# Seven tiles of a q-k product as three single-pass products from high and low parts, with the low parts made on GpSimd

## The chip, the cores and the metric

One core of one Trainium2 chip runs the whole program. The metric is the device time of one execution in microseconds (us). PE is TensorE, DVE is VectorE, ACT is ScalarE, POOL is GpSimd, and SP is the queue that issues most of the loads.

## The reference

All inputs are float32. The core of what is computed:

```python
# q, k, v: (1, 6016, 256); tau: a number; w_in (256, 2048), w_out (2048, 256), twice
qn = q / (np.linalg.norm(q, axis=1, keepdims=True) + 1e-06)
kn = k / (np.linalg.norm(k, axis=1, keepdims=True) + 1e-06)
s = kn.transpose(0, 2, 1) @ qn / tau          # 256 x 256, a sum over 6016 tokens
a = softmax of s over its last axis
x = v @ a                                     # 6016 x 256
h = x @ w_in;  g = h * (1.0 / (1.0 + np.exp(-1.702 * h)));  y = g @ w_out
h = y @ w2_in; g = np.where(h > 0.0, h, np.exp(np.minimum(h, 0.0)) - 1.0);  out = g @ w2_out
```

The norms run over the 6016 tokens, so a column of q or k has one norm, and the division by it can be made on the 256 x 256 product.

## The kernel before, in words

The program has two parts. The first, some 50 us long, loads q and k and makes the product, the norms and the softmax. The second, the long one, runs the two MLPs in units of 448 or 512 tokens; the change doesn't touch it. Each engine runs its instructions in the order in which the code writes them.

**The first part.** The 6016 tokens are 47 tiles of 128. `CHUNKS` cuts them into 17 chunks: 1, 2, 1, 2, 2, 2 tiles, then 3 and 4 alternately five times, then 2. Chunk 6 is the first of 3 tiles and chunk 7 the first of 4; chunk 16 is the last one. For a chunk, SP loads its q and k (`load_qk`), ACT squares both at once (L768), DVE adds the squares up (L638, through `sums`), and PE makes the product (L680, `gram`). The product s has two halves of 128 rows, each in a PSUM bank: `gram(i, c)` adds the tiles of chunk i to half c. Its operands are float32, and PE makes each of these products in two passes, each of them a record of its own in the trace.

- **The sums of squares.** From chunk 6 on, DVE folds a chunk's 3 or 4 tiles of squares into 2 (the sum into `sq`) and adds these into `pair` (128 x 1024). The squares lie in three buffers, so the squares of a chunk wait until the sums have read those three chunks back. From chunk 14 on, the additions into `pair` are made in halves of 512 columns, eight in all, and then two additions make `acc` (128 x 256 each for q and k).
- **The order on PE.** Up to chunk 11 both halves of a chunk are made at once. From chunk 12 on (`SPLIT`) half 0 is made for all five chunks, then half 1 of chunk 12 and of two tiles of chunk 13. Then stands `norms()` (L692): four tiny products that sum `acc` over the partitions. The rest of half 1 (11 tiles) and the transposes of v (L452) are written between the steps of the softmax, to fill PE while the other engines work.
- **The steps of the softmax.** `norms()` is read by an ACT copy (L696), a GpSimd power (L697, square roots of 4 columns) and DVE (L700, L701, reciprocals); PE then spreads the reciprocal norms of q over the partitions (L709, `rows_of_q`, it reads `rn`), and ACT copies that from PSUM to `rq` (L713). DVE multiplies half 0 by both norms (L719, `lowest(0)`), takes row minima (L723), ACT takes exponentials (L728), PE transposes them (L739), and the result is multiplied into the first weights (L541, `fold_half`). tau comes through L813 on PE and L702 on DVE. In the same places DVE and ACT unpack the weights of the MLP (L213, L217, L225, L228, L231, L267, L273).

GpSimd has, in the first 100 us, a few fills at the start and the power of 4 columns.

Of the kernel before, what the change touches and what calls it, by code (L numbers as in the profile page):

```python
# [9 lines left out]
F32 = mybir.dt.float32  # L10
# [7 lines left out]
P = 128  # L18
# [4 lines left out]
def kernel(  # L23
# [40 lines left out]
    nc = tc.nc  # L64
    _, NT, C = q.shape
# [3 lines left out]
    NJ = NT // P  # L69
# [11 lines left out]
    SPLIT = 12  # L81
# [48 lines left out]
    def x_tile(kind, b, i):  # L130
        x_t[kind, b, i] = xp.tile([P, 2, BANK], F32R, tag=f"x{i}", name=f"x{kind}")
        return x_t[kind, b, i]
# [237 lines left out]
    def do(f, n):  # L370
        f(n)
        if f in (split, split_lo):
            state["done"] = n
# [237 lines left out]
    with tc.manual_schedule():  # L611
        make_identity(nc, ident)

        with ExitStack() as st:
# [11 lines left out]
            starts = [sum(CHUNKS[:i]) for i in range(NC)]  # L626
            MM = max(CHUNKS)
            s_ps = bank[:KC]

            qk = [wts.tile([P, 14 * C], F32, tag=f"wA{i}", name="qk") for i in range(4)]  # L630

            def warm_up(n):
                for _ in range(n):
                    one = nc.const_aps.tensor(1.0, [P, P], F32)
                    nc.tensor.matmul(bank[3][:, :P], one, one, start=True, stop=True)  # L635

            def add(out, x, y):
                return lambda: nc.vector.tensor_add(out, x, y)  # L638

            def halves(y):  # L640
                return [add(pair[:, x], pair[:, x], y[:, x]) for x in range(2)]

            def sums(i, sq):

                m = CHUNKS[i]
                if i < 3:
                    kept.append(sq)
                    if not i:
                        return []
                    lone, two = kept[i - 1 and 2], kept[1]  # L650
                    return [add(pair[:, :, i - 1, :], two[:, :, i - 1, :], lone[:, :, 0, :])]
                a = sq[:, :, :2, :]
                if i in (3, 4, 5):
                    return [add(pair, pair, a)]
                if i == NC - 2:
                    return halves(a) + halves(sq[:, :, 2:, :])
                if m == 4:
                    return [add(a, a, sq[:, :, 2:, :]), add(pair, pair, a)]
                if m == 3:
                    x = sq[:, :, 0, :]  # L660
                    if i == NC - 3:
                        return [add(x, x, sq[:, :, 2, :])] + halves(a)
                    return [add(x, x, sq[:, :, 2, :]), add(pair, pair, a)]
                return halves(a) + [
                    add(acc[:, x], pair[:, x, 0, :], pair[:, x, 1, :]) for x in range(2)
                ]
# [6 lines left out]
            rk = ph1.tile([P, KC], F32, name="rk")  # L673
            rq_ps = bank[3][:, C:]
            e, rq = pair[:, 0], pair[:, 1, 0, :]

            def gram(i, c, cut=slice(None)):
                t = chunk[i]
                for s in range(CHUNKS[i])[cut]:
                    nc.tensor.matmul(  # L680
                        s_ps[c][:, :C],
                        t[:, 1, s, c * P:(c + 1) * P],
                        t[:, 0, s, :],
                        start=(starts[i] + s == 0),
                        stop=(starts[i] + s == NJ - 1),
                    )

            def norms():
                for i in range(2):
                    for c in range(KC):  # L690
                        x = i * KC + c
                        nc.tensor.matmul(  # L692
                            n_ps[:, x:x + 1], acc[:, i, c * P:(c + 1) * P], ones[:, 0:1],
                            start=True, stop=True,
                        )
                nc.scalar.copy(rn, n_ps[:, :2 * KC])  # L696
                nc.gpsimd.tensor_tensor(rn, rn, half, op=ALU.pow)  # L697
# [9 lines left out]
            def rows_of_q():  # L707
                for c in range(KC):
                    nc.tensor.matmul(  # L709
                        rq_ps[:, c * P:(c + 1) * P], rn[:, c:c + 1].to_broadcast([P, P]), ident,  # L710
                        start=True, stop=True,
                    )
                nc.scalar.copy(rq, rq_ps)  # L713

            mn = ph1.tile([P, KC], F32, name="mn")
            sm = ph1.tile([P, KC], F32, name="sm")

            def lowest(c):
                nc.vector.scalar_tensor_tensor(  # L719
                    out=e[:, c, :], in0=s_ps[c][:, :C], scalar=rk[:, c:c + 1], in1=rq,  # L720
                    op0=ALU.mult, op1=ALU.mult,
                )
                nc.vector.tensor_reduce(  # L723
                    mn[:, c:c + 1], e[:, c, :], axis=AX.X, op=ALU.min
                )

            def exps(c):
                nc.scalar.activation(  # L728
                    e[:, c, :], e[:, c, :], AF.Exp, bias=mn[:, c:c + 1], scale=-1.0,
                    accum_out=sm[:, c:c + 1],  # L730
                )
# [17 lines left out]
            def load_qk(i):  # L749
                m, a = CHUNKS[i], i % 2  # L750
                t = qk[i // 2 % 4][:, :8 * C] if a else qk[i // 2 % 4][:, 8 * C:]
                t = t.rearrange("p (x s c) -> p x s c", x=2, c=C)
                j = starts[i]
                nc.sync.dma_start(out=t[:, 0, :m, :], in_=qv[:, j:j + m, :])
                (nc.scalar if i < 3 else nc.sync).dma_start(out=t[:, 1, :m, :], in_=kv[:, j:j + m, :])
                return t
# [3 lines left out]
            chunk = []  # L760
            warm_up(6)
            for i, m in enumerate(CHUNKS):
                t = first[i] if i < 4 else load_qk(i)
                chunk.append(t)
                sq = gp.tile([P, 2, MM, C], F32, tag="g", name="sq")
                cuts = (slice(0, 2), slice(2, m)) if i == NC - 2 else (slice(0, m),)
                for x in cuts:
                    nc.scalar.activation(sq[:, :, x, :], t[:, :, x, :], AF.Square)  # L768
                todo += sums(i, sq)
                if todo:  # L770
                    todo.pop(0)()
                while len(todo) > 1:
                    todo.pop(0)()
                if i < SPLIT:
                    for c in range(KC):
                        gram(i, c)
                if i == 0:
                    warm_up(1)
# [13 lines left out]
            def turn_v(c, h):  # L792
                transpose_v(0, h, c, bank[4 + 2 * h + c])

            for i in range(SPLIT, NC):
                gram(i, 0)
            gram(SPLIT, 1)
            gram(SPLIT + 1, 1, slice(0, 2))
            do(scale, 0)
# [2 lines left out]
            do(join, 0)  # L802
            do(sign, 0)
            do(shift, 1)
            norms()
            turn_v(0, 0)
            gram(SPLIT + 1, 1, slice(2, None))
# [6 lines left out]
            inverse()  # L814
            do(split_lo, 0)
            rows_of_q()
            gram(SPLIT + 2, 1, slice(2, None))
            gram(SPLIT + 3, 1, slice(0, 3))
            turn_v(0, 1)
            do(scale_low, 2)  # L820
            lowest(0)
            exps(0)
            do(sign, 1)
            sums_inverse(0)
# [6 lines left out]
            gram(SPLIT + 4, 1)  # L831
            fold_half(0, 0, bank[3][:, :C])
            lowest(1)
            half_out(0, 0, bank[3][:, :C], 0)
            exps(1)
# [616 lines left out]
        for t in range(len(units) + 1):  # L1452
            u = units[t] if t < len(units) else None
            if u:
                kind, b, p = u
# [78 lines left out]
```

## Time and profile before

| what | value |
|---|---|
| runs of the kernel before | 1036.75, 1037.41, 1037.40 us; median 1037.4 |
| profiled execution, its own time | 1035.95 us |
| its span in the trace | 1034.2 us |
| PE busy over the span | 1029.1 us |
| DVE, ACT, POOL busy | 830.0, 755.9, 65.6 us |
| granted clock of TensorE | 1.00 in every stretch |

The span is what the trace shows from its first to its last instruction; 1.75 us of the execution lie outside it. Ends of matmuls are modelled by the profiler, so PE's busy time says that it is never long without work, and the chain of waits says where it waited.

### The profile page before, as it was taken

Reading aid. Unit: us, or ns where it says so; the run is one execution under the profiler, and the core shown is the slowest. Engines: PE = TensorE matmul, PEld = TensorE weight load, DVE = VectorE, ACT = ScalarE, POOL = GpSimd, SP = SyncE. Lnnn points to the kernel's source line nnn. Section 1 sums busy time; section 2 is a strip of 40 time slices with the busy share of each in tenths; the row PEclk is TensorE's granted clock in tenths of the full one; section 3 lists DMA queues with packets and bytes.
Section 4 is the critical chain, followed back from the end, with each engine's and each line's share of the span. In section 5 each row is a group of like instructions: output and inputs, shape, how many; then the busy total and the mean of one; then the engine's idle time right before and its main releaser. Section 6 shows DMA issues by size and latency. Waiting matters only on the chain.

```text
span 1034.2 us, 13723 instructions
## 1 busy us (share of the span) xinstructions
PE 1029.1 (100%) x4784; PEld 871.3 (84%) x4784; DVE 830.0 (80%) x1352; ACT 755.9 (73%) x1418; POOL 65.6 (6%) x118
## 2 busy tenths in 40 slices
PE   9999999999999999999999999999999999999998
PEld 8899988888888888888888888888888888888998
DVE  6888877757768777767348999998998998998897
ACT  6687676777677677777567878777777777777875
POOL 0000111102102111111000000000000000000000
PEclk9999999999999999999999999999999999999999
DMA  9852663356485586474573132123114024014021
GB/s 361 305 155 61 209 210 112 146 190 223 146 304 188 177 312 228 126 283 183 223 260 127 41 109 96 21 30 155 34 28 143 4 35 145 1 29 138 1 31 47
DMA packets 127543, 145.22 MB, mean 140 GB/s; under 512 B 91218, under 2 KB 94722, under 8 KB 126962
## 3 DMA queue, kind: packets, MB, share of 16 engines
q1 hardware_dynamic: 111554, 87.39, 27.4%
q0 software_dynamic: 15344, 56.17, 14.5%
q8 instruction: 37, 0.61, 0.2%
q10 hardware_dynamic: 576, 0.79, 0.2%
q14 instruction: 32, 0.26, 0.1%
HBM read 86.70 MB, written 57.61 MB: 140 GB/s over the span
## 4 chain that ended last, share of the span: by engine, by line
PE 99%; DMA 0%; ACT 0%; issue 0%
PE b L993 46%; PE b L892 40%; PE b L680 4%; PE b L1020 4%; PE b L583 4%; PE b L541 1%; DMA qk<-in_k_dram 0%; PE b L452 0%; PE b L692 0%; PE b L709 0%; PE b L739 0%; ACT ob L1058 0%; PE b L813 0%; PE b L635 0%
## 5 line engine op out<-in xcount | busy, mean ns | idle before, releaser
L993 PE MATMUL b<-g,wBA 128*128 128x512 f32 (+1 forms) x1152 | 295.9, 385 | 0.0
L892 PE MATMUL b<-xB,wAB 128*128 128x512 f32 (+1 forms) x1008 | 263.7, 385 | 0.0
L993 PEld LDWEIGHTS b<-g,wBA 128*128 128x128 f32 x1152 | 216.2, 188 | 41.1 <-DVE wBA L273 0.3
L993 PE MATMUL b<-g,wBB 128*128 128x512 f32 x960 | 250.1, 389 | 0.0
L892 PE MATMUL b<-xA,wAA 128*128 128x512 f32 x840 | 223.1, 389 | 0.0
L892 PEld LDWEIGHTS b<-xB,wAB 128*128 128x128 f32 x1008 | 187.0, 188 | 34.9 <-DVE b L1311 0.3
L993 PEld LDWEIGHTS b<-g,wBB 128*128 128x128 f32 x960 | 180.0, 188 | 37.5
L892 PEld LDWEIGHTS b<-xA,wAA 128*128 128x128 f32 x840 | 157.6, 188 | 32.9 <-ACT b L1298 0.4
L951 ACT CAST g<-gg 128x512 fp32r<-128x512 f32 (+1 forms) x192 | 117.0, 617 | 81.9 <-DVE gg L944 79.1
L939 DVE SCALAR_TENSOR_TENSOR ee<-ee,th 128x512 f32<-128x512 f32 (+1 forms) x192 | 129.7, 675 | 22.3 <-ACT th L929 22.2
L922 ACT ACTIVATE g<-b 128x512 fp32r<-128x512 f32 (+1 forms) x152 | 89.8, 591 | 75.2 <-PE b L892 66.9
L955 DVE TENSOR_TENSOR g<-gf,g 128x512 fp32r<-128x512 f32 (+1 forms) x192 | 129.1, 674 | 14.6 <-ACT gf L923 14.6
L1311 DVE TENSOR_TENSOR b<-b,s 128x512 f32<-128x512 f32 (+1 forms) x88 | 60.9, 692 | 93.1 <-PE b L892 88.2
L955 DVE TENSOR_TENSOR g<-gg,g 128x512 fp32r<-128x512 f32 (+1 forms) x192 | 127.6, 670 | 5.7 <-ACT g L951 4.1
L928 ACT ACTIVATE ee<-b 128x512 f32<-128x512 f32 (+1 forms) x144 | 84.8, 589 | 35.2 <-PE b L892 35.0
L944 DVE SCALAR_TENSOR_TENSOR gg<-b,ee 128x512 f32<-128x512 f32 (+1 forms) x144 | 98.0, 680 | 5.0
L923 ACT ACTIVATE gf<-b 128x512 f32<-128x512 f32 (+1 forms) x152 | 89.4, 588 | 3.2 <-DVE g L955 3.2
L929 ACT ACTIVATE th<-b 128x512 f32<-128x512 f32 (+1 forms) x144 | 84.1, 584 | 0.0
L1305 ACT COPY s<-b 128x512 f32<-128x512 f32 (+1 forms) x88 | 51.8, 589 | 27.1 <-PE b L892 27.0
L1330 DVE TENSOR_TENSOR c<-b,s 128x512 f32<-128x512 f32 (+1 forms) x88 | 59.8, 679 | 14.7 <-PE b L892 14.4
L1298 ACT COPY b<-b 128x512 f32<-128x512 f32 (+1 forms) x88 | 51.6, 586 | 13.5 <-PE b L892 13.2
L1020 PE MATMUL b<-wBB,g 128*128 128x256 f32 x336 | 46.2, 283 | 0.0
(111 smaller groups left out, 897.0 us busy)
## 6 DMA issues: line engine op xcount, KB each, us to landing
xdA<-xt POOLq DMA_DIRECT2D x35, 512.0 KB, 3.2
xA<-xdA SPq DMA_DIRECT2D x35, 512.0 KB, 5.7
xdB<-xt POOLq DMA_DIRECT2D x35, 512.0 KB, 3.5
xB<-xdB SPq DMA_DIRECT2D x35, 512.0 KB, 5.5
wAB<-w3d SPq DMA_DIRECT2D x4, 1792.0 KB, 8.4
v_raw<-in_v_dram SPq DMA_DIRECT2D x160, 32.0 KB, 2.4
out_dram<-ob SPq DMA_DIRECT2D x160, 32.0 KB, 1.7
raw<-in_moe_w_in_dram SPq DMA_DIRECT2D x8, 512.0 KB, 7.6
```

What stands on the lines that cost most here:

```text
L892: nc.tensor.matmul(dst[:, :n], w[:, wi, p % 2, WOP[kind][i], :], x[:, xi, :n], start=(start and k == 0), stop=(k == 2), skip_group_check=True,
L922: nc.scalar.activation(self.sl(ik)[0], h, AF.Gelu_apprx_sigmoid)
L923: nc.scalar.activation(t[:, :n], h, AF.Gelu_apprx_sigmoid)
L928: nc.scalar.activation(e[:, :n], h, AF.Exp)
L929: nc.scalar.activation(t[:, :n], h, AF.Tanh, scale=0.5)
L939: nc.vector.scalar_tensor_tensor(out=e[:, :n], in0=e[:, :n], scalar=1.0, in1=t[:, :n], op0=ALU.add, op1=ALU.mult,)
L944: nc.vector.scalar_tensor_tensor(out=g[:, :n], in0=h, scalar=0.0, in1=e[:, :n], op0=ALU.max, op1=ALU.min)
L951: nc.scalar.copy(self.sl(ik)[0], self.tmp[ik][:, :self.n])
L955: nc.vector.tensor_sub(lo, self.tmp.pop(ik)[:, :self.n], hi.bitcast(F32))
L993: nc.tensor.matmul(bank[a][:, :n], w[:, f, wi, d * P:(d + 1) * P], g[:, gi, k * n:(k + 1) * n], start=fresh((kind, b, a)), stop=(p == NP - ...
L1020: nc.tensor.matmul(bank[a][:, x * C:(x + 1) * C], g[:, gi, s * P:(s + 1) * P], w[:, f, wi, :], start=fresh((kind, b, a)), stop=(p == NP - ...
L1311: nc.vector.tensor_add(bank[c][:, :n], bank[b][:, :n], s5[:, :n])
```

## The change

Seven tiles (`SPLITS` lists chunk and tile) no longer go through the float32 product. ACT copies q and k of the tile (512 columns) to a single-pass type, the high part; GpSimd subtracts this from the float32 values, which gives the low part; PE makes three single-pass products: high by high, high by low, low by high. The parts lie in seven buffers that the second part of the program uses later (`x_tile`, `SLOTS`). In chunks 8 to 11 ACT's copies stand ahead of the squares of the chunk, in chunk 12 behind them. One of DVE's sums into `sq`, that of chunk 14, goes to GpSimd. ACT copies half 0 of the product to SBUF ahead of the norms, `lowest(0)` reads that copy and the spread norms straight from PSUM, and the copy to `rq` moves behind `lowest(0)`.

```diff
@@ sums
                     if i == NC - 3:
-                        return [add(x, x, sq[:, :, 2, :])] + halves(a)
+                        nc.gpsimd.tensor_add(x, x, sq[:, :, 2, :])
+                        return halves(a)
@@
+            SPLITS = [(8, 2), (9, 2), (9, 3), (10, 2), (11, 2), (11, 3), (12, 2)]
+            SLOTS = [0, 4, 5, 1, 3, 6, 2]
+            split_t = {}
+
+            def split_qk(i):
+
+                for n, (x, s) in enumerate(SPLITS):
+                    if x != i:
+                        continue
+                    y = split_t[i, s] = x_tile("qk", n, SLOTS[n])
+                    hi, lo = (y[:, a, :].rearrange("p (x c) -> p x c", c=C) for a in range(2))
+                    src = chunk[i][:, :, s, :]
+                    nc.scalar.copy(hi, src)
+                    nc.gpsimd.tensor_sub(lo, src, hi.bitcast(F32))
@@ gram
-                    nc.tensor.matmul(
-                        s_ps[c][:, :C],
-                        t[:, 1, s, c * P:(c + 1) * P],
-                        t[:, 0, s, :],
-                        start=(starts[i] + s == 0),
-                        stop=(starts[i] + s == NJ - 1),
-                    )
+                    y = split_t.get((i, s))
+                    terms = [(t[:, 1, s, r], t[:, 0, s, :])]
+                    if y is not None:
+                        k = [y[:, a, C:][:, r] for a in range(2)]
+                        x = [y[:, a, :C] for a in range(2)]
+                        terms = [(k[0], x[0]), (k[0], x[1]), (k[1], x[0])]
+                    for n, (a, b) in enumerate(terms):
+                        nc.tensor.matmul(
+                            s_ps[c][:, :C], a, b,
+                            start=(starts[i] + s == 0 and n == 0),
+                            stop=(starts[i] + s == NJ - 1 and n == len(terms) - 1),
+                        )
@@ rows_of_q
-                nc.scalar.copy(rq, rq_ps)
@@ lowest
+                x, y = (s_ps[1][:, :C], rq) if c else (e[:, 0, :], rq_ps)
                 nc.vector.scalar_tensor_tensor(
-                    out=e[:, c, :], in0=s_ps[c][:, :C], scalar=rk[:, c:c + 1], in1=rq,
+                    out=e[:, c, :], in0=x, scalar=rk[:, c:c + 1], in1=y,
@@ the loop over chunks
+                if i < SPLIT:
+                    split_qk(i)
                 cuts = (slice(0, 2), slice(2, m)) if i == NC - 2 else (slice(0, m),)
                 for x in cuts:
                     nc.scalar.activation(sq[:, :, x, :], t[:, :, x, :], AF.Square)
+                if i >= SPLIT:
+                    split_qk(i)
@@ behind the loop
             do(shift, 1)
+            nc.scalar.copy(e[:, 0, :], s_ps[0][:, :C])
             norms()
@@
             lowest(0)
+            nc.scalar.copy(rq, rq_ps)
             exps(0)
```

On ACT, chunks 8 to 12 of the changed program (`xqk` is the tile of high and low parts, `sq` the squares, `qk` a chunk as loaded; the line numbers of the changed program are higher):

```order
L690 CAST xqk_224<-qk_131 128x512
L792 ACTIVATE sq_223<-qk_131 128x2x768
L690 CAST xqk_243<-qk_131 128x512
L690 CAST xqk_246<-qk_131 128x512
L792 ACTIVATE sq_242<-qk_131 128x2048
L690 CAST xqk_271<-qk_132 128x512
L792 ACTIVATE sq_270<-qk_132 128x2x768
L690 CAST xqk_290<-qk_132 128x512
L690 CAST xqk_293<-qk_132 128x512
L792 ACTIVATE sq_289<-qk_132 128x2048
```

Before, only the `sq` rows stood there, back to back; now six copies stand between them, and a seventh behind the squares of chunk 12.

On GpSimd, from the fills at the start to the first loads that it issues (here `rn` holds the norms):

```order
 L621 MEMSET ones 128x128
 L622 MEMSET half 128x4
-L697 TENSOR_TENSOR rn<-rn,half 128x4
+L691 TENSOR_TENSOR xqk<-qk,xqk 128x512 x7
+L662 TENSOR_TENSOR sq<-sq 128x2x256
+L719 TENSOR_TENSOR rn<-rn,half 128x4
 L188 DMA raw<-in_moe_w_in_dram 128x1024 x2
```

Eight instructions of 512 columns, each with two inputs in SBUF, now stand ahead of the power.

On DVE, the end of the sums of squares, from chunk 13 on:

```order
 L638 TENSOR_TENSOR sq<-sq 128x2x512
 L638 TENSOR_TENSOR pair<-pair,sq 128x1024
-L638 TENSOR_TENSOR sq<-sq 128x2x256
 L638 TENSOR_TENSOR pair<-pair,sq 128x512 x8
 L638 TENSOR_TENSOR acc<-pair 128x256 x2
```

The sum of chunk 14 is gone from DVE, and the first of the eight halves waits for GpSimd instead.

## Rows read from the trace of the kernel before

**Rows 1.** The page: PE's busy time, and the chain that ended last, by engine.

```profile
PE 1029.1 (100%) x4784; PEld 871.3 (84%) x4784; DVE 830.0 (80%) x1352; ACT 755.9 (73%) x1418; POOL 65.6 (6%) x118
PE 99%; DMA 0%; ACT 0%; issue 0%
```

**Rows 2.** The chain of waits, 0 to 50 us: start us, length us, what.

```profile
5.45 34.97 PE b L680 x162
40.42 0.79 PE b L692 x8
...
43.73 0.64 PE b L709 x4
...
46.54 0.35 PE b L739 x2
46.89 1.30 PE b L680 x6
48.18 0.71 PE b L541 x6
```

**Rows 3.** The same view near the end: products of 256 columns, single-pass.

```profile
963.05 1.43 PE b L1020 x12
```

**Rows 4.** The timeline of DVE: start us, length us, instruction, count, idle time before it.

```profile
31.44 1.23 DVE L638 TENSOR_TENSOR sq<-sq 128x1024 f32<-128x1024 f32 x1 [1.04 <-ACT sq L768]
32.70 1.22 DVE L638 TENSOR_TENSOR pair<-pair,sq 128x1024 f32<-128x1024 f32 x1
33.84 0.68 DVE L638 TENSOR_TENSOR sq<-sq 128x512 f32<-128x512 f32 x1
34.56 4.91 DVE L638 TENSOR_TENSOR pair<-pair,sq 128x512 f32<-128x512 f32 x8
39.38 0.76 DVE L638 TENSOR_TENSOR acc<-pair 128x256 f32<-128x256 f32 x2
40.04 0.43 DVE L225 TENSOR_SCALAR bits<-raw 128x512 int32<-128x512 int32 x1
...
41.34 0.69 DVE L231 SCALAR_TENSOR_TENSOR bits<-raw,bits 128x512 int32<-128x512 int32 x1
...
42.51 0.69 DVE L228 CUSTOM_DVE_ANT_0 bits<-raw,bits 128x1024 uint16<-128x1024 uint16 x1
...
43.32 0.18 DVE L701 RECIPROCAL rn<-rn 128x4 f32<-128x4 f32 x1
43.77 0.17 DVE L702 RECIPROCAL rtau<-b 128x1 f32<-128x1 f32 x1 [0.28 <-PE b L813]
...
44.82 0.48 DVE L719 SCALAR_TENSOR_TENSOR pair<-b,rk,pair 128x256 f32<-128x256 f32 x1
```

**Rows 5.** The timeline of ACT.

```profile
19.43 3.45 ACT L768 ACTIVATE sq<-qk 128x2048 f32<-128x2048 f32 x2 [1.08 <-DVE pair L638]
23.95 1.91 ACT L768 ACTIVATE sq<-qk 128x2048 f32<-128x2048 f32 x1 [1.08 <-DVE pair L638]
26.92 1.49 ACT L768 ACTIVATE sq<-qk 128x1536 f32<-128x1536 f32 x1 [1.06 <-DMA qk<-in_k_dram]
29.49 3.44 ACT L768 ACTIVATE sq<-qk 128x2048 f32<-128x2048 f32 x2 [1.08 <-DMA qk<-in_k_dram]
...
42.07 0.62 ACT L267 CAST w1s<-bits 128x512 fp32r<-128x512 f32 x1 [0.67 <-DVE bits L231]
42.60 0.53 ACT L462 CAST xA<-b 128x448 fp32r<-128x448 f32 x1
...
44.41 0.37 ACT L713 COPY pair<-b 128x256 f32<-128x256 f32 x1 [0.72 <-PE b L709]
```

**Rows 6.** The timeline of GpSimd, 0 to 50 us.

```profile
1.02 0.29 POOL masks.py:199 TENSOR_SCALAR_AFFINE_SELECT ident<-ident 128x128 f32<-128x128 f32 x1
...
1.41 0.10 POOL L622 MEMSET half<- 128x4 f32 x1
41.55 1.39 POOL L697 TENSOR_TENSOR rn<-rn,half 128x4 f32<-128x4 f32 x1 [40.05 <-ACT rn L696]
```

More of the change, by code (lines that the diff above doesn't have):

```diff
@@ L675 @@
             e, rq = pair[:, 0], pair[:, 1, 0, :]
+            SPLITS = [(8, 2), (9, 2), (9, 3), (10, 2), (11, 2), (11, 3), (12, 2)]
[10 more added lines that the diff above has]
+                    nc.gpsimd.tensor_sub(lo, src, hi.bitcast(F32))
             def gram(i, c, cut=slice(None)):
                 t = chunk[i]
+                r = slice(c * P, (c + 1) * P)
                 for s in range(CHUNKS[i])[cut]:
-                    nc.tensor.matmul(
-                        s_ps[c][:, :C],
-                        t[:, 1, s, c * P:(c + 1) * P],
-                        t[:, 0, s, :],
-                        start=(starts[i] + s == 0),
-                        stop=(starts[i] + s == NJ - 1),
-                    )
+                    y = split_t.get((i, s))
[10 more added lines that the diff above has]
+                        )
             def norms():
```

## The prediction

> **What bounds the kernel now.** I read the page first. PE is busy for 1029.1 of 1034.2 us, and the chain that ended last lies on PE for 99% of the span [rows 1]. So a product that PE need not make is worth its time, unless another engine then comes late. Second, the chain in order of time [rows 2]: from 5.45 to 40.42 us PE makes q-k products without a break, 162 records in 34.97 us, and after that it goes from step to step of the softmax with hardly a gap. Third, who stands close behind PE there: the timeline of DVE [rows 4]. The second addition into `acc` ends at 39.38 + 0.76 = 40.14 us, and PE begins the norms that read `acc` at 40.42 [rows 2, 4]. From L225 at 40.04 to L701 at 43.32 DVE works almost without a pause, `rn` is there at 43.50, and PE begins to spread it (L709) at 43.73 [rows 2, 4]. DVE is thus within 0.3 us of being the bound at both places. That is the point of the whole case: PE can gain in this stage only what DVE gains too.
>
> **What PE saves.** A record of the float32 product takes 34.97 / 162 = 0.216 us, a product is two records, 0.432 us [rows 2]. A single-pass product of 256 columns takes 1.43 / 12 = 0.119 us near the end of the program [rows 3], and 0.71 / 6 = 0.118 in L541 [rows 2]. Three of them cost 0.358 us, which is 0.074 less than one float32 product. Seven tiles in two halves are 14 products: 14 x 0.074 = 1.0 us. All 14 stand ahead of the norms, so PE would reach the norms at 39.4 instead of 40.42.
>
> **Are the parts there in time?** A copy of 512 columns on ACT costs 0.53 us from start to start (42.07 to 42.60) [rows 5]. GpSimd's price for 512 columns with two inputs is not in the trace. Its rows give 0.29 us for 128 columns with one input and 0.10 for 4 columns [rows 6], hence 0.19 for each further 128 columns read. With one stream that makes 0.10 + 4 x 0.19 = 0.86, with two streams read in turn 0.10 + 8 x 0.19 = 1.62 us. I take the middle, 1.2, and keep both ends. PE makes a tile (both halves) in 0.864 us, so it comes to chunk 8's split tile at about 5.45 + 16 x 0.864 + 0.86 = 20.1 us, to chunk 11's second at about 28.5 and to chunk 12's at about 31.3. ACT's copies of these end at about 17.4, 25.5 and 29.4 (next part), GpSimd's last difference 1.2 us later, chunk 11's at 27.4 because two queue there. Even at 1.62 us each (19.1, 28.2, 31.0) PE does not wait. No cost here.
>
> **What the copies do to ACT and DVE.** ACT has a pause of about 1.08 us ahead of nearly every pair of squares [rows 5], and the copies fill it. Chunk 9 has landed by 19.43 at the latest. Two copies push its squares (1.91 us) to 20.5 to 22.4; a copy and 1.49 us of squares bring chunk 10 to 24.4; two copies and 1.91 bring chunk 11 to 27.4 (before: 25.86); chunk 12's squares end at 28.9 and its copy at 29.4. Chunk 13 starts at 29.49 as before, and ACT is level again [rows 5]. DVE's sums cost, from start to start, 1.26 (sum of 4 tiles), 1.14 (addition into `pair`) and 0.72 (sum of 3 tiles) [rows 4]. Chunk 11's sum can start at 27.4, so chunk 12's starts at 29.8, chunk 13's at 31.7 (before: 31.44), and chunk 13's addition ends its turn at 34.1. There the sum of chunk 14 stood (33.84); it is gone, so the eight halves can begin at 34.1 instead of 34.56, some 0.45 us earlier. They wait for GpSimd's sum: chunk 14's squares end at 29.49 + 3.44 = 32.93 [rows 5], and 1.2 us later is 34.13, just in time. The change thus spends nearly all of what DVE sheds (0.72) and the idle 1.04 us ahead of 31.44 on the late squares, and keeps 0.45.
>
> **The sum.** The additions into `acc` end at 39.7, so PE finds them ready at 39.4 to 39.8, and the norms end 1.0 us earlier than before. But `rn` hangs on DVE, which moves by 0.45 only: L709 starts at 43.73 - 0.45 = 43.28, though PE would be there at 42.73. PE waits 0.55 us and 0.45 of the 1.0 is kept. Behind that DVE gains a little more: its 0.28 us of waiting for tau (L702) vanishes, since PE makes that product early [rows 4]. `lowest(0)` could then start at 44.82 - 0.73 = 44.1. The copy to `rq`, 0.37 us on ACT [rows 5], would have allowed 44.33; the spread norms in PSUM are there at 43.28 + 0.64 = 43.92 [rows 2], so here the rewritten `lowest` helps. The exponentials come 0.73 us earlier, the transposes L739 no longer wait for them (at most 0.1 us of their 0.35 [rows 2]), and PE reaches L541 about 0.5 us before 48.18. The extra copy of half 0 on ACT costs nothing: ACT idles ahead of the norms, and PE needs neither. Were that cover gone it would cost its 0.37 us. Behind 48 us the chain is PE's own work again, and a shift of 0.5 us stays. The profiled execution took 1035.95 us, so 1035.45; the median of the runs lies 1.45 above it, so the forecast is **1036.9 us**. Its own range is a gain of 0.3 to 1.0, 1036.4 to 1037.1. A difference of 0.2% (2.07 us) is about what a measurement of this kernel tells from none, so this counts as no change.
>
> **Rival 1, the end on the other side: GpSimd and DVE shut each other out.** All eight new GpSimd instructions read two tiles in SBUF, while DVE runs one addition with two SBUF inputs after the other. If only one of the two engines can run such an instruction at a time, DVE loses 8 x 1.2 = 9.6 us. Its pauses under the forecast between chunk 8 and the halves take up about 2.2 of that, and the 0.45 and 0.28 above are lost; `acc` and everything behind it come 6.7 us later than before, and PE stands: 1044 us, with the ends 0.86 and 1.62 from 1041.4 to 1047.5. It turns into "slower" once each instruction takes more than about 0.3 us from DVE. For it: nothing in the trace shows DVE and GpSimd both streaming. Against it: the power on GpSimd spans 41.55 to 42.94, L231 (two SBUF inputs) runs from 41.34 into it and L228 starts within it at 42.51, and each takes 0.69 us [rows 4, 6]. That is weak, since the power reads only 4 columns. The Trainium skill, SBUF — State Buffer, section Who interferes with whom, says that a Vector instruction with two SBUF inputs contends with a GpSimd instruction that reads SBUF, by an exclusive lock held for the whole instruction. By that rule the sum would be the 1044 of this rival; the row just told does not agree with a lock over the whole span. I give it 0.19.
>
> **Rival 2, a shared port.** Both go on, each more slowly. If DVE loses half of GpSimd's time, 4.8 us, less the 2.2 of pauses and half of the gain, the end comes 2 to 3 us later: 1039.8, between 1038 and 1041.3. Same evidence; 0.12.
>
> **Rival 3, the change does nothing.** GpSimd's price is the upper end. Its sum of chunk 14 then ends at 32.93 + 1.62 = 34.55, the halves start at 34.56 as before, and PE's 1.0 us turns into waiting at the norms and at L709: 1037.3. For it: the margin in the forecast is nil at 1.2 us. 0.12.
>
> **How the numbers follow.** Forecast 0.54, rival 1 0.19, rival 2 0.12, rival 3 0.12, and 0.03 for a gain over 0.2%, which no row carries, since PE sheds 1.0 us in all. Faster 0.03; same 0.54 + 0.12 + the 0.03 of rival 2 that stays below 2.07 us, 0.69; slower 0.28. The range runs from 1035.9 (all of the 1.0 kept, and half a us of spread between runs) to 1041.3 (all of rival 2): it leaves out rival 1 and the large gain, about 0.2.
>
> **What would show it.** Right: 42 single-pass records in the place of 28; the additions of `acc` end at 39.7; PE idles about half a us at L709; GpSimd's eight instructions last about 1.2 us each and DVE's additions keep 0.69 and 1.23 us. Wrong, if DVE's additions grow longer or wait for GpSimd, if the first of the eight halves starts later than 34.6, or if PE waits for a low part ahead of chunk 12.

## The result, and the profile after

The changed kernel takes 1045.34 us (median of 5 runs, 1044.29 to 1045.75) against 1037.09 for the kernel before (5 runs, 1036.27 to 1037.41). The ratio is 1.0081, 95% interval 1.0069 to 1.0092: slower by 0.8%. The profiled execution took 1045.34 us too, with a span of 1043.6. It was rival 1 that came (1044, between 1041.4 and 1047.5), and not the forecast of 1036.9.

The page of the changed kernel, busy times and the chain by engine, against [rows 1]:

```profile
PE 1033.0 (99%) x4798; PEld 874.2 (84%) x4798; DVE 837.4 (80%) x1351; ACT 759.5 (73%) x1426; POOL 78.8 (8%) x126
PE 95%; DVE 3%; DMA 1%; ACT 0%; issue 0%; SPq 0%; ACTq 0%; DVEq 0%
```

DVE has one instruction less and is busy 7.4 us longer, and the chain that ended last, which was 99% PE, now lies on DVE for 3% of the span. So one looks at how long DVE's instructions last. The timeline of DVE in the changed kernel, against [rows 4]:

```profile
18.06 2.18 DVE L638 TENSOR_TENSOR pair<-pair,sq 128x1024 f32<-128x1024 f32 x1
20.16 1.77 DVE L638 TENSOR_TENSOR sq<-sq 128x512 f32<-128x512 f32 x1
...
30.32 1.23 DVE L638 TENSOR_TENSOR pair<-pair,sq 128x1024 f32<-128x1024 f32 x1
31.47 2.31 DVE L638 TENSOR_TENSOR sq<-sq 128x1024 f32<-128x1024 f32 x1
...
36.81 2.29 DVE L638 TENSOR_TENSOR sq<-sq 128x1024 f32<-128x1024 f32 x1
39.14 6.24 DVE L638 TENSOR_TENSOR pair<-pair,sq 128x1024 f32<-128x1024 f32 x9
45.29 0.76 DVE L638 TENSOR_TENSOR acc<-pair 128x256 f32<-128x256 f32 x2
...
48.43 0.69 DVE L228 CUSTOM_DVE_ANT_0 bits<-raw,bits 128x1024 uint16<-128x1024 uint16 x1
```

And the timeline of GpSimd in the same stretch, against [rows 6]:

```profile
17.50 1.66 POOL L691 TENSOR_TENSOR xqk<-qk,xqk 128x512 fp32r<-128x512 f32 x1 [15.99 <-ACT xqk L690]
20.05 3.01 POOL L691 TENSOR_TENSOR xqk<-qk,xqk 128x512 fp32r<-128x512 f32 x2 [0.90 <-ACT xqk L690]
23.52 1.76 POOL L691 TENSOR_TENSOR xqk<-qk,xqk 128x512 fp32r<-128x512 f32 x1 [0.46 <-ACT xqk L690]
26.06 3.69 POOL L691 TENSOR_TENSOR xqk<-qk,xqk 128x512 fp32r<-128x512 f32 x2 [0.77 <-ACT xqk L690]
30.76 1.93 POOL L691 TENSOR_TENSOR xqk<-qk,xqk 128x512 fp32r<-128x512 f32 x1 [1.02 <-ACT xqk L690]
36.68 1.35 POOL L662 TENSOR_TENSOR sq<-sq 128x512 f32<-128x512 f32 x1 [3.98 <-ACT sq L792]
47.98 1.22 POOL L719 TENSOR_TENSOR rn<-rn,half 128x4 f32<-128x4 f32 x1 [9.95 <-ACT rn L718]
```

Read the two side by side. An addition of 1024 columns that meets no GpSimd instruction keeps 1.23 us, as at 30.32; one that meets one lasts 2.18 to 2.31, and a sum of 512 columns 1.77 in place of 0.69. There are eight such additions for the eight GpSimd instructions, each longer by 0.95 to 1.08 us, 8.2 us in all. Of that DVE's shorter pauses take up 1.4 (its waits for squares from 13.8 us on fall from 3.6 us to 2.2) and the sum it no longer makes 0.7; 6.1 remain. `acc` is complete at 46.05 in place of 40.14, 5.9 us late.

The ends of the rows show that the two engines take turns. GpSimd's first difference ends at 17.50 + 1.66 = 19.16, and the addition that began at 18.06 ends 1.08 us later, at 20.24. The other way round, the addition of 30.32 ends at 31.55, and the difference that began at 30.76 ends 1.14 us later, at 32.69. So it is in all eight meetings: an addition of 1024 columns ends 1.08 us after GpSimd's instruction, a sum of 512 columns 0.55 us after it, and GpSimd's instruction 1.13 to 1.15 us after DVE's. The rows of both engines grow, because they contain the wait for the other.

The timeline of PE shows the two places where it stood, ahead of a low part and ahead of the norms:

```profile
29.80 0.50 PE L704 MATMUL b<-xqk 128*128 128x256 f32 x2 [0.73 <-POOL xqk L691]
...
45.77 1.87 PE L714 MATMUL b<-ones,acc 128*128 128x1 f32 x8 [4.83 <-DVE acc L638]
```

The chain of waits of the changed kernel from there, against [rows 2]:

```profile
45.77 1.87 PE b L714 x8
...
48.59 3.41 PE b L704 x8
...
52.52 1.05 PE b L731 x4
53.57 1.73 PE b L704 x8
...
57.25 0.71 PE b L541 x6
```

L714 is the norms (before L692), L731 spreads the reciprocal norms (before L709). PE reaches L541 at 57.25 in place of 48.18, 9.07 us later, which is the whole loss of the profiled execution (1045.34 - 1035.95 = 9.4) but for 0.3. Of this, 5.35 us are there when the norms begin (45.77 in place of 40.42). The other 3.72 lies in PE's own rows from there to L541: the norms last 1.87 us in place of 0.79, and the eight records of the q-k product at 48.59 last 3.41 in place of 1.73, which is also what the next eight take at 53.57. The view by stretches (length, busy us and records of PE, PEld, DVE, ACT, POOL, then the granted clock, the DMA share and GB/s) says why:

```profile
40.00:50.00 10.00, 5.17 (x21) 4.45 (x20) 9.04 (x18) 5.77 (x11) 1.22 (x1) 0.65 0.50 197
50.00:60.00 10.00, 10.00 (x52) 8.38 (x52) 6.18 (x16) 4.20 (x12) 0.00 (x0) 0.83 0.04 6
```

PE was without work for 4.83 us ahead of the norms, and the granted clock, 1.00 in every stretch of before, is 0.65 and 0.83 in these two. The eight records took 0.426 us each, twice the 0.216 of before, so PE ran at the lower of its levels (1.2 GHz) and came back to 2.4 GHz by 53.57.

### The profile page after: what moved, and what is told of

It is laid out like the page before. It is cut to its first block, busy times and chain, and to the rows that moved or that the text cites. A ratio compares the mean times of both kernels' runs of the same rounds, so it can differ in the third digit from the quotient of the medians.

```text
span 1043.6 us, 13777 instructions
## 1 busy us (share of the span) xinstructions
PE 1033.0 (99%) x4798; PEld 874.2 (84%) x4798; DVE 837.4 (80%) x1351; ACT 759.5 (73%) x1426; POOL 78.8 (8%) x126
## 4 chain that ended last, share of the span: by engine, by line
PE 95%; DVE 3%; DMA 1%; ACT 0%; issue 0%; SPq 0%; ACTq 0%; DVEq 0%
PE b L1021 45%; PE b L920 40%; PE b L1048 4%; PE b L583 4%; DVE pair L638 1%; DVE sq L638 1%; DMA qk<-in_k_dram 1%; PE b L541 1%; PE b L704 1%; PE b L452 0%; ACT sq L792 0%; PE b L714 0%; PE b L731 0%; ACTq L777 0%; SPq L776 0%
## 5 line engine op out<-in xcount | busy, mean ns | idle before, releaser
L492 POOL DMA_DIRECT2D xdB<-xt x42 | 23.8, 567 | 299.7 <-ACT g L979 165.3
```

## The experiments

**Theory A.** An addition on DVE with two inputs in SBUF and a GpSimd instruction that reads two tiles in SBUF shut each other out for most of GpSimd's time; the wait that this gives PE then lets its clock fall. **Rivals.** The copies: ACT's copies hold up the squares, and DVE is late for that reason. The products: the low parts come too late for PE, or the single-pass products cost more than they save. The busy neighbour: GpSimd slows DVE whatever their operands.

**1. No low parts** (`e1_no_low`: the products take the high part three times; GpSimd's sum of chunk 14 stays)

```diff
-                    nc.gpsimd.tensor_sub(lo, src, hi.bitcast(F32))
...
-                        terms = [(k[0], x[0]), (k[0], x[1]), (k[1], x[0])]
+                        terms = [(k[0], x[0]), (k[0], x[0]), (k[0], x[0])]
```

> The low parts aren't made and the three products read the high parts instead, so the low parts are left out of the result; ACT's seven copies, the 42 single-pass products and GpSimd's sum of chunk 14 stay. Theory A (GpSimd and DVE exclude each other): DVE's additions between 17 and 31 us go back to 1.23 and 0.69 us, only the one beside GpSimd's sum of chunk 14 stays long, PE waits under 1 us at the norms, 1036.5 to 1038. Theory B (ACT's copies delay the squares, and with them DVE): the wait at the norms stays at 4 to 5 us, 1043 or more.

1037.93 us, ratio 1.0019 (1.0010 to 1.0029). All additions up to 33 us have 1.23 and 0.69 us again, with ACT's copies and all 42 single-pass products in place. One of them in the timeline of DVE:

```profile
27.95 1.23 DVE L638 TENSOR_TENSOR sq<-sq 128x1024 f32<-128x1024 f32 x1 [1.21 <-ACT sq L791]
```

7.4 of the 8.3 us are gone with seven GpSimd instructions: the copies and the single-pass products fall as the main cause. 0.8 to 1.1 us remain; experiment 7 turns to them.

**2. GpSimd fills the low parts with zeros** (`e2_fill_low`: seven GpSimd instructions of the same size that read nothing)

```diff
-                    nc.gpsimd.tensor_sub(lo, src, hi.bitcast(F32))
+                    nc.gpsimd.memset(lo.bitcast(F32), 0.0)
```

> GpSimd fills the low parts with zeros instead of subtracting, so the low parts are left out of the result; all else as in the change, the same eight instructions on GpSimd, seven of them reading nothing. If it is the reading on GpSimd that shuts DVE out: DVE's additions keep 1.23 and 0.69 us except beside the sum of chunk 14, 1036.5 to 1038. If any GpSimd instruction does, or the handing over between ACT, GpSimd and PE: 1042 or more.

1037.75 us, ratio 1.0014 (1.0005 to 1.0024). But the fills did not run beside the additions. A fill waits for no copy of ACT, and GpSimd made all seven at the start (the timeline of GpSimd), while DVE's first addition begins at 7.06:

```profile
1.44 3.29 POOL L691 MEMSET xqk<- 128x512 f32 x7
```

So this run repeats experiment 1, the change without GpSimd's reading beside DVE's additions, and does not test the busy neighbour. Experiment 5 has fills beside additions.

**3. DVE makes the low parts itself** (`e3_dve_low`)

```diff
-                    nc.gpsimd.tensor_sub(lo, src, hi.bitcast(F32))
+                    nc.vector.tensor_sub(lo, src, hi.bitcast(F32))
```

> DVE makes the low parts itself, GpSimd only the sum of chunk 14. DVE gets 7 x 0.72 = 5.0 us more work, of which about 2 go into pauses. Theory A: each difference on GpSimd cost DVE about 1.0 us, so its own 0.72 is cheaper: acc about 2 to 3 us later than in the kernel before, and less clock lost, 1039 to 1042. Theory C (the port is only shared, the loss is elsewhere): as slow as the change or slower, 1045 or more.

1040.36 us, ratio 1.0038 (1.0023 to 1.0052). The timeline of DVE shows what a difference costs there, and what is left of the meeting with GpSimd (the sum of chunk 14):

```profile
18.26 0.69 DVE L691 TENSOR_TENSOR xqk<-qk,xqk 128x512 fp32r<-128x512 f32 x1
...
33.49 2.30 DVE L638 TENSOR_TENSOR sq<-sq 128x1024 f32<-128x1024 f32 x1
```

A low part costs DVE 0.69 us if it makes it, and 1.03 if GpSimd makes it beside an addition. Handing this work to the idle engine took more of the busy one than doing it there.

**4. The change with PE kept at work ahead of the norms** (`e4_keep_clock`: twenty spare products whose result nobody reads)

```diff
+            warm_up(20)
             norms()
```

> The change with 20 products of constants (128 columns, float32, about 0.22 us each) ahead of the norms, so that PE works while it waits for acc. If the fall of TensorE's clock behind the wait is a cost of its own: the granted clock stays at 1.00 between 40 and 60 us, the products behind the norms go back to their old lengths, 3 to 3.7 us less than the change, 1041.5 to 1042.5. If the long records there are waiting for operands: no difference, 1045.

1043.92 us, ratio 1.0069 (1.0054 to 1.0084), 1.4 us below the change in the medians and above the range expected. The intervals of the two ratios overlap, so the profile has to decide. The stretch of the wait, and L541 in the chain of waits:

```profile
40.00:50.00 10.00, 9.52 (x71) 8.66 (x70) 9.51 (x21) 5.70 (x11) 1.17 (x1) 1.00 0.49 193
```

```profile
53.99 0.71 PE b L541 x6
```

The clock stays at 1.00 (from 50 to 60 us too) and PE reaches L541 3.26 us earlier than in the change, with `acc` as late as there (46.19). So of the 9.07 us in the profiles 3.26 are the clock's and 5.8 DVE's lateness. The runs give back less (two at 1043.0, two at 1044.9); why the latter two are longer, no profile shows.

**5. The pairs by themselves** (`m1_pairs`: a small program, six instructions of each kind on one or both engines, no part of this kernel)

```diff
+        def two(n=2 * N):
+            nc.vector.tensor_add(vc[:, :n], va[:, :n], vb[:, :n])
...
+        def one_psum():
+            nc.vector.tensor_add(vc[:, :N], bk, vb[:, :N])
...
+        def scaled():
+            nc.vector.tensor_scalar(vc[:, :N], va[:, :N], 3.0, None, op0=ALU.mult)
...
+        def pool_two():
+            nc.gpsimd.tensor_sub(pc, pa, pb)
...
+        def pool_copy():
+            nc.gpsimd.tensor_copy(pc, pa)
```

`two` is L97, `one_psum` L100 (`bk` lies in PSUM, all else in SBUF), `scaled` L103, `pool_two` L106, `pool_copy` L112; L109 fills `pc`.

> A program of its own that leaves the whole computation out and copies q to the output: seven stages of up to six DVE and six GpSimd instructions side by side, in this order: GpSimd differences of 512 columns alone; DVE additions of 1024 columns with two SBUF inputs alone; both together; DVE additions of 512 columns with one input in PSUM beside the differences; DVE two-input additions beside GpSimd fills; the same beside GpSimd one-input copies; DVE one-input multiplications of 512 columns beside the differences. Theory A (one at a time): together the third stage takes about 6 x (1.23 + 1.15) = 14 us, records of either engine near 2.3 us; with one input in PSUM and beside fills both keep their own lengths (0.69, 1.23). Theory C (a shared port, both run on): in the third stage both records grow by a part and overlap, 9 to 11 us in all. For the one-input copies and multiplications no theory here has a number; if the second reading port is the cause, the copies exclude the two-input additions too.

The timeline of both engines, six instructions to a row: GpSimd alone, DVE alone, then the pairs.

```profile
23.25 7.96 POOL L106 TENSOR_TENSOR pc<-pa,pb 128x512 f32<-128x512 f32 x6
...
31.86 7.52 DVE L97 TENSOR_TENSOR vc<-va,vb 128x1024 f32<-128x1024 f32 x6
...
40.08 12.23 DVE L97 TENSOR_TENSOR vc<-va,vb 128x1024 f32<-128x1024 f32 x6
40.19 13.23 POOL L106 TENSOR_TENSOR pc<-pa,pb 128x512 f32<-128x512 f32 x6
...
53.95 4.31 DVE L100 TENSOR_TENSOR vc<-bk,vb 128x512 f32<-128x512 f32 x6
...
54.25 7.97 POOL L106 TENSOR_TENSOR pc<-pa,pb 128x512 f32<-128x512 f32 x6
...
62.86 7.53 DVE L97 TENSOR_TENSOR vc<-va,vb 128x1024 f32<-128x1024 f32 x6
62.90 3.43 POOL L109 MEMSET pc<- 128x512 f32 x6
...
71.10 8.96 DVE L97 TENSOR_TENSOR vc<-va,vb 128x1024 f32<-128x1024 f32 x6
71.21 9.33 POOL L112 COPY pc<-pa 128x512 f32<-128x512 f32 x6
```

GpSimd's difference takes 7.96 / 6 = 1.33 us alone, DVE's addition 1.25. Side by side both stretch, and the two sets end after 13.3 us; one whole instruction after the other they would take 15.5. The single rows alternate as in the kernel: each addition ends 1.08 us after a difference, each difference 1.12 after an addition, and six such pairs are the 13.3 us. With one of DVE's inputs in PSUM neither feels the other (4.31 / 6 = 0.72; 7.97). Beside fills the additions last 7.53, as alone (7.52), so it is not GpSimd's being busy: that rival falls. All this is theory A without the kernel around it, except that the two do not exclude each other for quite the whole length of an instruction.

The last stage had no number from theory A: DVE's multiplication of 512 columns with one input, in SBUF, beside differences. Its group by shape (shortest, median and longest in ns, first and last start in us):

```profile
L103 DVE TENSOR_SCALAR vc<-va x6: 426/1366/1369, 81.2 to 87.3; 128x512 f32<-128x512 f32 x6
```

The first, which began ahead of GpSimd, lasted 0.43 us, the other five 1.37. Having only one input in SBUF is thus not enough: this instruction was shut out too, which the addition with one input in SBUF and one in PSUM was not.

**6. Three tiles in place of seven** (`e8_three_tiles`)

```diff
-            SPLITS = [(8, 2), (9, 2), (9, 3), (10, 2), (11, 2), (11, 3), (12, 2)]
-            SLOTS = [0, 4, 5, 1, 3, 6, 2]
+            SPLITS = [(8, 2), (9, 2), (10, 2)]
+            SLOTS = [0, 4, 1]
```

> Three split tiles (the third of chunks 8, 9 and 10) in the place of seven, the sum of chunk 14 on GpSimd as in the change. Theory A: four additions on DVE are longer by about 1.0 us each in the place of eight, of which 1 to 2 us go into pauses, and PE's wait at the norms and the fall of the clock are smaller or absent: 1037.5 to 1039.5. If the loss came from one place (the last chunk's low part, or the sum of chunk 14) and not by the number of instructions: 1043 or more, or no loss at all.

1040.55 us, ratio 1.0032 (1.0023 to 1.0042), 1 us above the range expected. Four GpSimd instructions, four longer additions in the timeline of DVE:

```profile
19.80 2.18 DVE L638 TENSOR_TENSOR pair<-pair,sq 128x1024 f32<-128x1024 f32 x1
21.90 1.77 DVE L638 TENSOR_TENSOR sq<-sq 128x512 f32<-128x512 f32 x1
...
24.85 2.30 DVE L638 TENSOR_TENSOR sq<-sq 128x1024 f32<-128x1024 f32 x1
...
34.45 2.30 DVE L638 TENSOR_TENSOR sq<-sq 128x1024 f32<-128x1024 f32 x1
...
42.93 0.75 DVE L638 TENSOR_TENSOR acc<-pair 128x256 f32<-128x256 f32 x2
```

Half the instructions, half the loss on DVE (4.2 of 8.2 us); `acc` is 3.5 us late, PE waits 2.40 us at the norms, and the granted clock of 40 to 50 us is 0.83. Of the 10 runs the four at 1038.5 to 1039.0 us, with a granted clock of 0.999, lie in the range; the six above it, 1040.3 to 1042.1, have 0.996 to 0.998.

**7. The copies and the products alone, the rewrite alone, the sum alone.** `e7_copies_alone` has no new GpSimd instruction (high parts only, DVE makes the sum of chunk 14). `e5_edit_only` has `SPLITS = []` and that sum on DVE, so only the copies of half 0 and `rq` differ from before. `e6_sum_only` is `e5_edit_only` with the sum on GpSimd. `e12_copies_fill` is `e7_copies_alone` with six spare products ahead of the norms.

```diff
# e7_copies_alone: as experiment 1, and
-                        nc.gpsimd.tensor_add(x, x, sq[:, :, 2, :])
-                        return halves(a)
+                        return [add(x, x, sq[:, :, 2, :])] + halves(a)
# e12_copies_fill: the same, and
+            warm_up(6)
             norms()
```

> As the run without low parts (they are left out of the result), and the sum of chunk 14 is on DVE again, so GpSimd has no new instruction. Theory A: no addition on DVE is longer than 1.23 us, acc ends within 0.5 us of the kernel before, 1036.3 to 1037.3. Theory B (ACT's copies alone cost): over 1038.

> No tile is split and the sum of chunk 14 is on DVE; only the rewritten first row minimum (half 0 copied to SBUF, the spread norms read from PSUM) is left of the change. Every theory: within 0.5 us of the kernel before, 1036.3 to 1037.3, since DVE's weights stand ahead of it in either. If it costs by itself: over 1038.

> GpSimd makes the sum of squares of chunk 14, and nothing else of the change is there. Theory A: one VectorE instruction is about 1 us longer beside it, which eats what VectorE is spared; 1036.8 to 1038.5 us. The rival (the sum is a gain, only the low parts cost): 1036.3 to 1036.8 us with the accumulation 0.7 us earlier.

> The copies on ScalarE and the three single-pass products without any GpSimd instruction, with six spare products put in TensorE's queue ahead of the norms. If the two lengths of that kernel without spare products come from the clock, which falls in some executions in TensorE's short wait ahead of the norms: one length, 1036.5 to 1037.5 us, and a granted clock of 1.00 in every run. If they come from something else: the same spread up to 1040 us.

The rewrite alone: 1036.90 us, 0.9998 (0.9989 to 1.0007). The sum alone: 1037.00 us, 0.9997 (0.9988 to 1.0006). In the latter the meeting took another form than expected: DVE's addition had begun first and kept its length, GpSimd's sum took 2.05 us, and DVE waited for it.

```profile
33.20 2.05 POOL L662 TENSOR_TENSOR sq<-sq 128x512 f32<-128x512 f32 x1 [31.69 <-ACT sq L792]
```

```profile
32.89 1.22 DVE L638 TENSOR_TENSOR pair<-pair,sq 128x1024 f32<-128x1024 f32 x1
35.28 4.91 DVE L638 TENSOR_TENSOR pair<-pair,sq 128x512 f32<-128x512 f32 x8 [1.17 <-POOL sq L662]
```

The 1.17 us of waiting is more than the 0.72 that DVE was spared: this part of the change gains nothing by itself.

The copies alone: 1038.64 us, 1.0016 (1.0007 to 1.0025). That is above the range expected and on the side of the rival (over 1038): the copies and the products do cost something, 1.75 us in the median (1036.89 for the kernel before, beside it). No addition is longer than 1.23 us. Here `acc` is complete at 40.63, 0.5 us later than before, and PE, sooner done, waits for it (the timeline of PE):

```profile
40.44 1.02 PE L712 MATMUL b<-ones,acc 128*128 128x1 f32 x8 [0.89 <-DVE acc L638]
```

The profiled run took 1036.97 us. The 11 runs lie in two groups: five at 1036.9 to 1038.3 us with a granted clock of 0.999 or 1.00, six at 1038.6 to 1040.5 with 0.997 or 0.998. With the spare products in that wait the kernel takes 1037.50 us (1036.55 to 1037.97; 1.0001, 0.9992 to 1.0010), with no run under 0.999. So what the copies cost is a fall of the clock in some executions, which work in the wait prevents; the longer group takes some 2.5 us more (medians 1037.1 and 1039.6). How long PE waits in those executions no profile shows. Experiments 1 and 2 show the same signs (waits of 1.04 and 1.73 us in their profiles, their longest runs at 0.997 and 0.998), so the same is likely for what they kept, but it was not tested there.

**8. The change with DVE's running sum in PSUM** (`e9_psum`, and its control `e10_psum_before`, the kernel before with the rewrite and that sum in PSUM). Two free banks hold `pair` in halves of 512 columns, so each addition into it reads one input from PSUM and one from SBUF; a chunk of 4 tiles is added by four additions of 512 columns, and a chunk of 3 tiles adds its odd tile by two of 256. GpSimd's eight instructions are those of the change.

```diff
+            pp = [bank[5].rearrange("p (s c) -> p s c", c=C), bank[7].rearrange("p (s c) -> p s c", c=C)]
...
-                return [add(pair[:, x], pair[:, x], y[:, x]) for x in range(2)]
+                return [add(pp[x], pp[x], y[:, x]) for x in range(2)]
...
-                    return [add(x, x, sq[:, :, 2, :]), add(pair, pair, a)]
-                return halves(a) + [
+                    return halves(a) + [
+                        add(pp[x][:, 0, :], pp[x][:, 0, :], sq[:, x, 2, :]) for x in range(2)
+                    ]
+                return [add(pair[:, x], pp[x], a[:, x]) for x in range(2)] + [
```

> The change with one difference: VectorE's running sum of the pair of squares lies in PSUM (two halves of 512 columns in banks 5 and 7), so that each of its additions has one input in PSUM and one in SBUF; GpSimd makes the low parts and the last sum as in the change. Theory A (two SBUF reads on VectorE and GpSimd's work shut each other out): the additions keep their length of about 1.2 us per 1024 columns, plus a few tenths for being cut in two, GpSimd's differences last about 1.33 us, the accumulation is at most 1 us late, and the time is 1036 to 1039.5 us. The rival (GpSimd slows VectorE whatever its operands, or the order of the queues costs the time): the additions are again about 1 us longer for each GpSimd instruction and the time is 1042 to 1046 us.

> The control of the last one: the running sum in PSUM, no tile in parts and nothing new on GpSimd. Both theories: within 0.5 us of the kernel before, 1036.4 to 1037.6 us; if halving the additions costs VectorE more than 1 us in all, up to 1038 us.

1036.27 us (1036.07 to 1038.11, 11 runs), 0.9996 (0.9986 to 1.0005); the control 1037.02 us, 0.9997 (0.9988 to 1.0007). The groups of DVE's line L638 and GpSimd's difference L695, both by shape (shortest, median and longest in ns, first and last start in us):

```profile
L638 DVE TENSOR_TENSOR b<-b,sq x38: 422/690/700, 14.0 to 37.5; 128x512 f32<-128x512 f32 x30, 128x256 f32<-128x256 f32 x8
L695 POOL TENSOR_TENSOR xqk<-qk,xqk x7: 1284/1287/1299, 17.7 to 29.7; 128x512 fp32r<-128x512 f32 x7
```

The same group of GpSimd in the change:

```profile
L691 POOL TENSOR_TENSOR xqk<-qk,xqk x7: 1327/1720/2274, 17.5 to 30.8; 128x512 fp32r<-128x512 f32 x7
```

And the end of it in the kernel with the sum in PSUM, `acc` in the timeline of DVE and L541 in the chain of waits:

```profile
39.26 0.75 DVE L638 TENSOR_TENSOR acc<-pair 128x256 f32<-128x256 f32 x2
```

```profile
47.82 0.71 PE b L541 x6
```

The same eight GpSimd instructions, in the same stretch, no longer lengthen a single addition, and they have one length themselves. `acc` is complete at 40.01 and PE reaches L541 at 47.82, 0.36 us ahead of before. 9.1 us of the change's time go with where DVE's running sum lies; that the rewriting itself gains nothing, the control shows. This version beats the changed kernel; against the kernel before, a difference can't be measured.

## Why the prediction was wrong

**The step that failed** stands in the part on ACT and DVE: "DVE's sums cost, from start to start, 1.26 [...], 1.14 [...] and 0.72", which led to "the eight halves can begin at 34.1". These durations were taken from a trace in which GpSimd did nothing, and carried into a program in which it reads SBUF beside them. Next to each of GpSimd's eight instructions they are about 1.03 us longer, and the first half begins at 40.47. The cost that failed is DVE's time per sum beside a reading GpSimd: 0 us more was put in, 1.03 was measured, eight times.

**Why rival 1 got only 0.19.** The evidence against it, DVE's rows beside the power on GpSimd, could not bear the weight, light as it was. In the changed kernel, where the exclusion is plain, that row looks the same: the power runs from 47.98 to 49.20, and the L228 that begins at 48.43 within it takes its 0.69 us. So a GpSimd instruction that reads 4 columns tells nothing of one that reads 512, and the trace of before held no evidence on this point. Then the rule should have decided. The Trainium skill, SBUF — State Buffer, section Who interferes with whom, says that a Vector instruction with two SBUF inputs contends with a GpSimd instruction that reads SBUF, not with one that only writes, and not if the Vector instruction has at most one SBUF input and runs outside the modes that use both ports. Here the runs agree on the first three points: 1.03 us more on each addition, nothing beside fills (experiment 5), nothing with one input in PSUM (experiments 5 and 8); in which mode the multiplication of experiment 5 ran, the trace does not show. Where the rule says that the lock is held for the whole instruction, the runs give turns of 1.08 us of an addition's 1.23 and of 1.13 of GpSimd's 1.27 to 1.33.

**Rival 1's 1044 was nearly right, in part by luck.** Its mechanism came. It lost 9.6 us on DVE (measured 8.2), took 2.2 up in pauses (measured 1.4), and put `acc` 6.7 us late (5.9). It left out that PE's clock falls in the wait, 3.26 us in the profiles; the 0.8 too much on `acc` hid part of that. Its remark that it turns into "slower" above 0.3 us for each instruction does not follow from its own terms: with 2.2 in pauses, 0.73 of gain lost and a line of 2.07 us, that takes (2.07 + 2.2 + 0.73) / 8 = 0.63 us. **Rival 2**, both engines running on more slowly, does not fit the turns: each instruction ends a fixed time after the other engine's.

**The terms of the forecast, one by one.** PE's saving is best read where PE never waits, in the chain of waits of the copies with spare products:

```profile
6.12 34.16 PE b L702 x176
```

The 14 records more than before (162 in 34.97 us [rows 2]) take 0.81 us less; the forecast had 1.0. GpSimd's price, taken as 1.2 between 0.86 and 1.62: 1.27 to 1.33 undisturbed (experiments 8 and 5). "PE does not wait" for the parts: wrong in the change, where the lengthened difference of chunk 11's second tile held PE for 0.73 us at 29.80; right with the sum in PSUM, where PE waits for no low part. The end: L541 0.5 us earlier; with the sum in PSUM, which changes DVE's sums too, it is 0.36. So the forecast described the change without the exclusion, and there it held: no gain that can be measured, as it said. The three signs of error that it named all came: DVE's longer additions, the first half at 40.47 and not by 34.6, and PE's wait for a low part ahead of chunk 12.

**What stays open.** Why GpSimd shuts out DVE's multiplication with one input in SBUF and not its addition with one input there and one in PSUM; how long PE waits in the longer executions of experiment 7; and why two of the four runs of experiment 4 are 1.9 us longer than the others at the same granted clock.

## What to carry to other kernels

Before giving work to an engine that looks idle, ask what it reads and what the busy engine reads at that time: GpSimd reading SBUF beside VectorE additions with both inputs in SBUF cost VectorE more (1.03 us) than doing the work itself (0.69). If the two must run side by side, put one of VectorE's inputs into PSUM, as it was done here with an accumulator. Before reading a run as a test of two instructions side by side, look in its trace whether they met: the fills of experiment 2 did not. And price a wait that TensorE gets by what follows it too: its clock fell in the wait of 4.83 us, and the products behind it took 0.426 us in place of 0.216.

## What the runs showed of the hardware

- DVE and GpSimd take turns, and the one that begins while the other has its turn is stretched: in the change DVE's additions (1.23 to 2.2 or 2.3 us) and most of GpSimd's differences (median 1.72, undisturbed 1.29); in `e6_sum_only`, where DVE's addition had begun first and DVE then waited for the result, GpSimd's sum alone (2.05, undisturbed 1.27).
- A DVE multiplication of 512 columns with one input, in SBUF, lasts 0.43 us when it begins ahead of GpSimd and 1.37 beside a difference (`m1_pairs`).
- A GpSimd copy with one input in SBUF costs an addition with two inputs there much less than a difference does: six additions take 8.96 us beside copies, 12.23 beside differences, 7.52 alone.
- The granted clock of 40 to 50 us was 0.83 in the profiles with 2.40 and 2.55 us without work ahead of the norms (`e8_three_tiles`, `e3_dve_low`), 0.65 in the one with 4.83, and 1.00 in those with 0.89, 1.04 and 1.73; of the other runs of the last three kernels some showed a lower clock. It stayed at 1.00 with spare products in the wait (`e4_keep_clock`, `e12_copies_fill`).
